# A 40-us tail of row tiles: identity passes moved ahead of the last mode, channel matmul first, spectra evacuated in two parts, a lag of three

## The chip, the cores and the metric

The kernel runs on one core of a Trainium2 chip. The metric is the device time of one execution in microseconds (us). The core's engines work side by side, each through its own instructions in program order: TensorE (PE, matrix passes), VectorE (DVE), ScalarE (ACT), GpSimd (POOL) and SyncE (SP), which here only issues DMAs. PE writes its results to PSUM, eight banks of 2 KB per partition; DVE and ACT move them from there to SBUF.

## The reference

Two stages follow each other. The first is sparse attention over batch 8, 8 heads, 576 positions, head size 64 (four heads with a local mask of 32 positions, four with a strided mask). Its output, seen as x of shape (8, 576, 512), goes into a spectral mixer:

```python
X = np.fft.rfft(x, axis=1)
Xr, Xi = (np.real(X[:, :n_modes]), np.imag(X[:, :n_modes]))        # 64 modes
Yr = np.einsum('bmd,mde->bme', Xr, w_r) - np.einsum('bmd,mde->bme', Xi, w_i)
Yi = np.einsum('bmd,mde->bme', Xr, w_i) + np.einsum('bmd,mde->bme', Xi, w_r)
Y[:, :n_modes] = Yr + 1j * Yi
y = np.fft.irfft(Y, n=S, axis=1)
u = x + y
return (u + np.maximum(u @ w_ch, 0.0)).astype(np.float32)
```

The mode weights w_r and w_i are 64 matrices of 512 x 512 each. The output is (8, 576, 512) in float32, 9.44 MB.

## The kernel before, in words

Every engine runs its instructions in the order in which the program text issues them; waits between engines are inserted where one reads what another writes, and PSUM accesses to the same bank of one tile are put in order. No planner reorders anything.

**The weight stream.** `w_fetch` (L181) has POOL issue two DMAs per mode and half of the channels, 256 KB each on arrival, 254 in all. They run from the start to about 402.5 us. `mode(slot, m)` does 16 small passes (L516, 128x16) for one mode. Slot 0 handles one half of the channels while the local attention runs, slot 1 the other half while `premix` runs. Eight modes share one PSUM tile y; after the eighth, L531 or L533 moves all eight to SBUF (slot 1 adds what slot 0 left and writes the spectra tile YT).

**Premix.** While slot 1 streams, `premix` computes for each row tile (b, t) the product x @ w_ch (into `v0`, through ACT L612) and a copy of x in row order (`xo`, through DVE L613). There are five row tiles per batch: t = 0 to 3 with 128 rows, and t = 4 with 64 rows, two batches of which share one tile. That makes 36 units in the tail: per batch (b,0), (b,1), then (b,4) for odd b, then (b,2), (b,3).

**Spectra.** For every 16 modes and four batches `spec_mm` transposes the spectra (L622, into tp) and multiplies them by w_ch (L625, into zp). `spec_out` then copies, per batch, 32 rows of zp to `zz` on ACT (L631) and 32 rows of tp to `yy` on DVE (L632). The last 16 modes can go through this only after mode 63; for them `spec_last` is called.

**The tail (L809 to L886).** New PSUM pools are opened: z with 2 banks, v with 3, u with 3. They take the place of the pools tp, sc, av and y, which are closed. A unit does, in this order:

- `unit_v0`: PE passes `v0` through the identity into a v bank (L827).
- `unit_v`: `rows_v` adds the inverse transform of `zz` (L638, for t = 4 two half passes L641); ACT takes relu of it into `rl` (L836). For the units of `pool_adds` (t = 1, 3, 4, except (7,3), 19 in all) POOL adds `xo` to `rl` (L839).
- `unit_u`: for the other 17 units PE passes `xo` through the identity into a u bank (L654); for all, the inverse transform of `yy` (L656, for t = 4 L659). DVE adds u and `rl` into `osb` (L851). SP issues the output DMA: one of 512 KB for two units (L865), two of 128 KB for t = 4 (L856), and single ones of 256 KB for the last two units (L860).

On PE the order is: three `unit_v0`, the last spectra, then for each i `unit_v0(i)` (from i = 3), `unit_v(i)`, `unit_u(i - 2)`. With three banks for v, the identity pass of unit i waits for the relu of unit i - 3; with three for u, unit i waits for the add of unit i - 3. `spec_out` of the next batch follows the unit with t = 1; the last spectra of batches 4 to 7 follow unit (3,1).

Of the kernel before, what the change touches and what calls it, by code (L numbers as in the profile page):

```python
# [12 lines left out]
AluOp = mybir.AluOpType  # L13
ACTF = mybir.ActivationFunctionType

B = 8
# [3 lines left out]
NM = 64  # L20
# [57 lines left out]
def kernel(  # L78
# [10 lines left out]
    nc = tc.nc  # L89
    PSUM = bass.MemoryType.PSUM  # L90
# [5 lines left out]
    pss = {}  # L96
    pctx = ctx.enter_context(ExitStack())

    def psum_pools(**bufs):
        pctx.close()  # L100
        pss.clear()
        for n, c in bufs.items():
            pss[n] = pctx.enter_context(
                tc.tile_pool(name="ps_" + n, bufs=c, space=PSUM)
            )

    def psum(kind, half=False):
        if half:
            return pss[kind].tile([128, 1024], F16, tag=kind, name=kind)
        return pss[kind].tile([128, 512], FP, tag=kind, name=kind)  # L110
# [15 lines left out]
    idn = cs["cI"]  # L126
# [8 lines left out]
    YS = {}  # L135
# [28 lines left out]
    w_chs = {}  # L164

    def w_fetch(n=1):
        for _ in range(n):
            i = len(w_tiles)
            if i >= 2 * NM:
                return  # L170
            half, m = 1 - i // NM, i % NM
            if i in GUEST:
                n, j = GUEST[i]
                if j == 0:
                    guests[n] = big.tile([128, 2, 4, DM], F16, tag=n, name="wt")
# [329 lines left out]
    def mode(slot, m):  # L505
        half = 1 - slot
        mi, mg = m % 8, m // 8
        if mi == 0:
            ypt[slot] = psum("y")
        yp = ypt[slot]  # L510
        yv = yp.rearrange("p (m e x) -> p m e x", m=8, e=4)
        wt = w_tiles[slot * NM + m]
        pr = ds(0, 128 if m else 64)
        for e in range(4):
            for c in range(4):
                nc.tensor.matmul(  # L516
                    yv[:, mi, e, :],
                    wt[pr, XC[c], ds(128 * e, 128)],
                    Xh[half][pr, c, :, :, m],
                    start=(c == 0),  # L520
                    stop=(c == 3),
                )
        if slot or m not in GUEST:
            w_fetch()
        if mi == 7:
            part = (slice(None), slice(None), mg // 2, slice(None), ds(8 * (mg % 2), 8))
            src = yp.rearrange("p (m e x) -> p e x m", m=8, e=4)
            if slot == 0:
                if m == 7:
                    spectra_tile("Y0")  # L530
                nc.scalar.activation(out=YS["Y0"][part], in_=src, func=ACTF.Copy)  # L531
            else:
                nc.vector.tensor_tensor(  # L533
                    out=YS["YT"][part], in0=src, in1=YS["Y0"][part], op=AluOp.add
                )
# [83 lines left out]
    def spec_mm(g, bq, tp, zp):  # L619
        for e in range(4):  # L620
            lhs = YS["YT"][:, e, g, ds(8 * bq, 8), :].rearrange("p x m -> p (x m)")
            nc.tensor.transpose(tp[:, ds(128 * e, 128)], lhs, idn)  # L622
        for e in range(4):
            lhs = YS["YT"][:, e, g, ds(8 * bq, 8), :].rearrange("p x m -> p (x m)")
            nc.tensor.matmul(  # L625
                zp, lhs, w_chs["n"][:, e, :], start=(e == 0), stop=(e == 3)
            )

    def spec_out(g, b, tp, zp):
        src, dst = ds(32 * (b % 4), 32), ds(32 * g, 32)  # L630
        nc.scalar.activation(out=zzs[b][dst], in_=zp[src, :], func=ACTF.Copy)  # L631
        nc.vector.tensor_copy(out=yys[b][dst], in_=tp[src, 0:512])  # L632
# [14 lines left out]
                skip_group_check=True,  # L647
            )

    def rows_u(b, t, up, add):  # L650
        cols = out_cols(t)
        if add:
            xo = xos[b][:, t, :] if t < 4 else xoh[b // 2]
            nc.tensor.matmul(up, idn, xo, start=True, stop=(t == 4))  # L654
        if t < 4:
            nc.tensor.matmul(up, cs["cA"][:, cols], yys[b], start=not add, stop=True)  # L656
            return
        for i in range(2):
            nc.tensor.matmul(  # L659
                up[ds(64 * i, 64), :],  # L660
                cs["cA"][:, cols],
                yys[b - 1 + i],
                start=not add,
                stop=True,
                skip_group_check=True,
            )
# [63 lines left out]
    dft(B - 1, 1)  # L730


    psum_pools(tp=2, sc=2, av=2, y=2)
    NMODES = [11, 9, 8, 8, 7, 7, 7, 7]
    for b in range(B):
        load(B + b + 3)
# [2 lines left out]
        ends = [lambda h=h: loc_scores(b, h, True) for h in (0, 2)]  # L739
# [8 lines left out]
        n = 0  # L748
        nm = NMODES[b]
        for mi in range(nm):  # L750
# [3 lines left out]
            n = upto  # L754
# [7 lines left out]
    xoh = [ptr.tile([128, DM], F16, name=f"xoh{i}") for i in range(4)]  # L762
    zzs = [ptr.tile([128, DM], F16, name=f"zz{i}") for i in range(B)]
    yys = [ptr.tile([128, DM], F16, name=f"yy{i}") for i in range(B)]
# [31 lines left out]
            spec_out(g, b, tp, zp)  # L796

    n = 0
    for m in range(NM):
        mode(1, m)  # L800
        upto = min(len(work), -(-len(work) * (m + 1) // 62))
        for w in work[n:upto]:
            w()
        n = upto
        if m >= 16 and m % 16 in (4, 8):
            spec(m // 16 - 1, 0 if m % 16 == 4 else 1)


    psum_pools(z=2, v=3, u=3)  # L809
    units = []  # L810
    for b in range(B):
        units += [(b, 0), (b, 1)]
        if b % 2:
            units.append((b, 4))
        units += [(b, 2), (b, 3)]
    held, vps, rls, osbs = {}, {}, {}, {}
    LAST = len(units) - 1

    def spec_last(bq):
        held[bq] = psum("z", half=True), psum("z")  # L820
        spec_mm(3, bq, *held[bq])

    def unit_v0(i):
        b, t = units[i]
        vps[i] = psum("v")
        v0 = v0s[b][:, t, :] if t < 4 else v0h[b // 2]
        nc.tensor.matmul(vps[i], idn, v0, start=True, stop=(t == 4))  # L827

    def unit_v(i):
        b, t = units[i]  # L830
        vp = vps.pop(i)
        rows_v(b, t, vp)
        if t % 2 == 0:
            rls[b, t] = rls[b, t + 1] = pw.tile([128, 2, DM], FP, tag="w", name="rl")
        rl = rls[b, t][:, t % 2, :]
        nc.scalar.activation(out=rl, in_=vp, func=ACTF.Relu)  # L836
        if pool_adds(b, t):
            xo = xos[b][:, t, :] if t < 4 else xoh[b // 2]
            nc.gpsimd.tensor_tensor(out=rl, in0=rl, in1=xo, op=AluOp.add)  # L839

    def pool_adds(b, t):
        return t in (1, 3, 4) and (b, t) != (B - 1, 3)

    def unit_u(i):
        b, t = units[i]
        up = psum("u")
        rows_u(b, t, up, add=not pool_adds(b, t))
# [3 lines left out]
        nc.vector.tensor_tensor(  # L851
            out=osb[:, t % 2, :], in0=up, in1=rls[b, t][:, t % 2, :], op=AluOp.add
        )
        if t == 4:
            for j in range(2):
                nc.sync.dma_start(  # L856
                    out[b - 1 + j, ds(512, 64), :], osb[ds(64 * j, 64), 0, :]
                )
        elif i >= LAST - 1:
            nc.sync.dma_start(  # L860
                out[b, ds(256, 256), :].rearrange("(p i) e -> p i e", i=2)[:, t % 2, :],
                osb[:, t % 2, :],
            )
        elif t % 2:
            nc.sync.dma_start(  # L865
                out[b, ds(128 * (t - 1), 256), :].rearrange("(p i) e -> p i e", i=2),
                osb,
            )

    for i in range(3):  # L870
        unit_v0(i)
    spec_last(0)
    spec_out(3, 0, *held[0])
    LAG = 2
    for i in range(len(units) + LAG):
        if i < len(units):
            b, t = units[i]
            if i > 2:
                unit_v0(i)
            unit_v(i)  # L880
            if t == 1 and b + 1 < B:
                if b + 1 == 4:
                    spec_last(1)
                spec_out(3, b + 1, *held[(b + 1) // 4])
        if i >= LAG:
            unit_u(i - LAG)  # L886


# [28 lines left out]
```

The softmax here doesn't subtract the row's maximum and nothing guards it: scores larger than these inputs give would overflow.

## Time and profile before

| | |
|---|---|
| median of 4 runs | 445.53 us (443.85 to 446.93) |
| profiled execution | 444.46 us, its span 442.7 us |
| weight DMAs | 81 MB with the inputs, to about 402.5 us |
| PE busy, whole span | 341.3 us (77%) |
| last mode starts | 402.60 us |
| first row pass (L638) | 407.11 us |
| last PE pass starts | 436.34 us |
| last DVE add ends | 437.93 us |
| last output DMA issued | 439.0 us |

The page says, for one profiled execution, how long each engine was busy, and cuts the span into 40 slices. The chain of waits goes back from the last instruction to what released each. The timeline lists an engine's instructions with their start, length and the idle time before. In these rows, "PE y L516 x16" is sixteen passes of line 516 into tile y; a length in the timeline includes the way through the array, so passes that start 0.216 us apart are shown as 0.38 us long. The granted clock is the share of full speed at which PE ran.

### The profile page before, as it was taken

To read this page: it belongs to the slowest core of one execution; us is meant where nothing else is said; L and a number is where in the kernel's file an instruction comes from. 1 tells how busy PE (TensorE), PEld (TensorE's weight loads), DVE (VectorE), ACT (ScalarE), POOL (GpSimd) and SP (SyncE) were. 2 spreads that over 40 slices of the span, in tenths; PEclk is the share of its full clock that TensorE was granted. 3 is DMA by queue.
4 is the path that set the end of the run, shared out by engine and by line. 5 is a ranking of instruction groups with operands and counts; after the bars stand their busy time and mean duration, and the time that the engine had idled before them with its cause. 6 is when DMAs were issued, how large, how long until landed. Compare 5 with 4: busy or idle time off the path is not lost.

```text
span 442.7 us, 12293 instructions
## 1 busy us (share of the span) xinstructions
PE 341.3 (77%) x5285; PEld 242.4 (55%) x5285; DVE 214.8 (49%) x461; ACT 187.9 (42%) x353; POOL 179.6 (41%) x326
## 2 busy tenths in 40 slices
PE   3878789769898795866865575978869787887994
PEld 2767677648676674654743344545545464543441
DVE  4787767835344424150511034345344543732895
ACT  2675667645554543343441311215114221332883
POOL 5243333433433443443443444434444444410773
PEclk9996889888898958595785568779577885978998
DMA  8999999999999999999999999999999999990687
GB/s 186 181 205 204 197 200 204 212 208 211 210 211 211 213 212 200 212 211 212 211 210 212 212 212 212 211 212 208 210 194 208 213 211 213 210 208 17 262 323 272
DMA packets 30758, 92.35 MB, mean 209 GB/s; under 512 B 5936, under 2 KB 6832, under 8 KB 30704
## 3 DMA queue, kind: packets, MB, share of 16 engines
q0 software_dynamic: 26608, 81.28, 93.9%
q1 hardware_dynamic: 3520, 9.90, 6.0%
q8 instruction: 42, 0.69, 0.6%
q10 hardware_dynamic: 576, 0.38, 0.3%
q14 instruction: 12, 0.10, 0.1%
HBM read 163.37 MB, written 9.44 MB: 390 GB/s over the span
## 4 chain that ended last, share of the span: by engine, by line
DMA 58%; PE 16%; issue 2%; ACT 1%; DVEq 0%; DVE 0%; ACTq 0%; POOLq 0%
DMA wt<-in_moe_w_i_dram 47%; DMA wt<-in_moe_w_r_dram 9%; PE y L516 3%; DMA qn<-in_k_dram 2%; PE v L827 2%; PE tp L364 2%; PE v L638 1%; PE u L656 1%; PE sc L410 1%; PE sc L426 1%; PE u L654 1%; PE y L483 1%; PE av L447 1%; PE z L625 1%; PE av L455 0%
## 5 line engine op out<-in xcount | busy, mean ns | idle before, releaser
L516 PE MATMUL y<-X,wt 128*128 128x16 f16 (+1 forms) x2048 | 82.8, 192 | 64.2 <-DMA wt<-in_moe_w_i_dram 62.5
L181 POOL DMA_DIRECT2D wt<-in_moe_w_r_dram x128 | 66.2, 517 | 128.3 <-DMA wt<-in_moe_w_r_dram 28.9
L516 PEld LDWEIGHTS <-wt 128*128 128x128 f16 (+1 forms) x2048 | 72.7, 103 | 77.3 <-issue 52.0
L181 POOL DMA_DIRECT2D wt<-in_moe_w_i_dram x126 | 65.1, 516 | 63.5 <-DMA wt<-in_moe_w_i_dram 39.0
L603 PE MATMUL sc<-w_cp,xT 128*128 128x512 f16 (+1 forms) x160 | 54.7, 473 | 0.7 <-DVE xT L575 0.7
L612 ACT ACTIVATE v<-sc 128x512 f16<-128x512 f32 x32 | 19.0, 597 | 82.3 <-PE sc L603 82.2
L440 ACT ACTIVATE PL<-sc 128x480 f16<-128x480 f32 (+1 forms) x48 | 27.4, 579 | 40.7 <-PE sc L426 39.4
L613 DVE COPY xo<-tp 128x512 f16<-128x512 f16 x32 | 22.1, 692 | 45.3 <-PE tp L611 45.3
L219 DVE TENSOR_TENSOR xb<-av,rec 90x256 f16<-90x256 f32 (+2 forms) x80 | 36.0, 450 | 2.8
L218 DVE RECIPROCAL rec<-av 90x4 f32<-90x4 f32 (+2 forms) x80 | 14.7, 183 | 43.1 <-PE av L455 30.0
L371 DVE COPY qT<-tp 128x576 f16<-128x576 f16 x16 | 12.1, 759 | 45.6 <-PE tp L364 41.5
L229 ACT ACTIVATE v<-tp 128x640 f16<-128x640 f16 (+1 forms) x24 | 19.4, 807 | 26.6 <-PE tp L398 23.5
L364 PE MATMUL tp<-cI_s,qn 64*64 64x64 f16 x864 | 26.2, 210 | 4.7 <-issue 3.0
L329 ACT ACTIVATE PS<-sc 90x360 f16<-90x360 f32 (+1 forms) x48 | 22.8, 489 | 9.3 <-PE sc L322 8.6
L851 DVE TENSOR_TENSOR osb<-u,rl 128x512 f32<-128x512 f32 x36 | 23.3, 687 | 6.0 <-ACT rl L836 3.0
L839 POOL TENSOR_TENSOR rl<-rl,xo 128x512 f32<-128x512 f32 x15 | 17.3, 1156 | 21.2 <-ACT rl L836 20.7
L364 PEld LDWEIGHTS <-qn 64*64 64x64 f16 x864 | 20.5, 122 | 9.8 <-issue 4.7
L603 PEld LDWEIGHTS <-xT 128*128 128x128 f16 (+1 forms) x160 | 15.0, 112 | 16.6 <-issue 8.3
L254 PE MATMUL tp<-cI_s,qn 72*128 72x72 f16 x256 | 15.4, 211 | 10.7 <-DMA qn<-in_v_dram 7.9
L483 PEld LDWEIGHTS <-xb 108*128 108x128 f16 (+2 forms) x176 | 17.2, 115 | 11.5 <-DVE xb L219 6.1
L410 PE MATMUL sc<-cMl_s,cI_s 128*128 128x480 f16 (+1 forms) x48 | 21.9, 456 | 1.6 <-ACT X L229 1.6
L611 PEld LDWEIGHTS <-xT 128*128 128x128 f16 (+1 forms) x160 | 15.1, 117 | 13.7 <-issue 7.9
(92 smaller groups left out, 650.4 us busy)
## 6 DMA issues: line engine op xcount, KB each, us to landing
wt<-in_moe_w_r_dram POOLq DMA_DIRECT2D x128, 256.0 KB, 9.4
wt<-in_moe_w_i_dram POOLq DMA_DIRECT2D x126, 256.0 KB, 9.6
out_dram<-osb SPq DMA_DIRECT2D x15, 512.0 KB, 2.8
qn<-in_v_dram POOLq DMA_DIRECT2D x16, 288.0 KB, 10.7
qn<-in_q_dram POOLq DMA_DIRECT2D x16, 288.0 KB, 10.9
qn<-in_k_dram POOLq DMA_DIRECT2D x16, 288.0 KB, 10.7
out_dram<-osb SPq DMA_DIRECT2D x8, 128.0 KB, 2.5
w_ch<-in_moe_w_ch_dram POOLq DMA_DIRECT2D x1, 512.0 KB, 11.7
```

The lines of the kernel that those rows point to most:

```text
L181: nc.gpsimd.dma_start(wt[ds(64 * ri, 64)], src[m, ds(256 * half, 256), :].rearrange("(p c) e -> p c e", c=4),)
L219: nc.vector.tensor_tensor(out=dst, in0=val.rearrange("p h (q c) -> p h c q", c=4), in1=rec[0:n, 0:pieces] .to_broadcast((n, pieces, 64)) . ...
L229: nc.scalar.activation(out=out, in_=in_, func=ACTF.Copy)
L329: nc.scalar.activation(out=PS[0:n, ds(POFF[t], 4 * n)], in_=scp[0:n, 0 : 4 * n], func=ACTF.Exp, scale=SCALE,)
L364: nc.tensor.transpose(tp[ds(64 * hp, 64), ds(64 * i, 64)], qn[ds(64 * hp, 64), vi, ds(64 * (9 * g + i), 64)], idn[ds(64 * hp, 64), ds(64 * ...
L410: nc.tensor.matmul(scp[:, 0 : n * times].rearrange("p (h x) -> p h x", h=times), idn, mask_rows("cMl", n, times), start=True, stop=False,)
L440: nc.scalar.activation(out=dst, in_=src, func=ACTF.Exp, scale=SCALE)
L483: nc.tensor.matmul(xp[:, ds(192 * cp, 192)], xb[b][0:n, base + t, ds(128 * cp, 128)], F[0:n, t, :], start=(i == 0), stop=(i == len(tiles) ...
L516: nc.tensor.matmul(yv[:, mi, e, :], wt[pr, XC[c], ds(128 * e, 128)], Xh[half][pr, c, :, :, m], start=(c == 0), stop=(c == 3),)
L603: nc.tensor.matmul(vp[pr, :], xT[:, ch, cols], w_chs["cp"][:, ch, :], start=(ch == 0), stop=(ch == 3),)
L613: nc.vector.tensor_copy(out=xo[pr].rearrange("p (h q c) -> p h q c", h=2, c=4), in_=tp[pr, 0:512].rearrange("p (h c q) -> p h q c", h=2, c=4),
L851: nc.vector.tensor_tensor(out=osb[:, t % 2, :], in0=up, in1=rls[b, t][:, t % 2, :], op=AluOp.add)
```

## The change

- `psum_pools` no longer forgets older pools. Pool y is opened first and stays open to the end; in the tail, v and u (3 banks each) take the place of tp, sc and av, and the last spectra use the two y banks.
- The eighth group of slot 1 is evacuated in two parts: six modes after the sixth, two after the eighth.
- The loop over modes stops at 62. Then three units do their identity passes for v and for u (`v_early`, `u_early`: six passes, as unit (0,1) is no longer added by POOL), and only then does mode 63 run.
- `spec_last` does the four channel matmuls first, then the four transposes.
- `pool_adds` leaves out (0,1) and adds (2,2) and (4,2): 20 units.
- `u_rows` follows `v_rows` at a distance of three units for i from 4 to 31, and of two before and after.
- The first two units send their output singly. The second half of the last t = 4 tile and the last unit's output are issued on ACT's queue.

```diff
@@ mode
-        if mi == 7:
-            part = (slice(None), slice(None), mg // 2, slice(None), ds(8 * (mg % 2), 8))
-            src = yp.rearrange("p (m e x) -> p e x m", m=8, e=4)
+        ends = {7: 8}
+        if slot and mg == 7:
+            ends = {5: 6, 7: 2}
+        if mi in ends:
+            n = ends[mi]
+            m0 = mi + 1 - n
...
+            src = yp.rearrange("p (m e x) -> p e x m", m=8, e=4)[:, :, :, ds(m0, n)]
@@ pools
-    psum_pools(tp=2, sc=2, av=2, y=2)
+    psum_pools()
+    pss["y"] = ctx.enter_context(tc.tile_pool(name="ps_y", bufs=2, space=PSUM))
+    psum_pools(tp=2, sc=2, av=2)
...
-    for m in range(NM):
+    for m in range(NM - 1):
...
-    psum_pools(z=2, v=3, u=3)
+    psum_pools(v=3, u=3)
@@ tail
+    def pool_adds(b, t):
+        if (b, t) in ((0, 1), (B - 1, 3)):
+            return False
+        return t in (1, 3, 4) or (b, t) in ((2, 2), (4, 2))
+
     def spec_last(bq):
-        held[bq] = psum("z", half=True), psum("z")
-        spec_mm(3, bq, *held[bq])
+        zp = psum("y")
+        tp = psum("y", half=True)
+        held[bq] = tp, zp
+        for dst in (zp, tp):
+            for e in range(4):
+                lhs = YS["YT"][:, e, 3, ds(8 * bq, 8), :].rearrange("p x m -> p (x m)")
+                if dst is tp:
+                    nc.tensor.transpose(tp[:, ds(128 * e, 128)], lhs, idn)
+                else:
+                    nc.tensor.matmul(
+                        zp, lhs, w_chs["n"][:, e, :], start=(e == 0), stop=(e == 3)
+                    )
+    def u_early(i):
         b, t = units[i]
+        ups[i] = psum("u")
+        if not pool_adds(b, t):
+            nc.tensor.matmul(ups[i], idn, x_rows(b, t), start=True, stop=(t == 4))
...
-                nc.sync.dma_start(
+                (nc.scalar if b == B - 1 and j else nc.sync).dma_start(
...
-        elif i >= LAST - 1:
-            nc.sync.dma_start(
+        elif i < 2 or i >= LAST - 1:
+            (nc.scalar if i == LAST else nc.sync).dma_start(
...
     for i in range(3):
-        unit_v0(i)
+        v_early(i)
+        u_early(i)
+    mode(1, NM - 1)
     spec_last(0)
     spec_out(3, 0, *held[0])
-    LAG = 2
-    for i in range(len(units) + LAG):
-        if i < len(units):
-            b, t = units[i]
-            if i > 2:
-                unit_v0(i)
-            unit_v(i)
-            if t == 1 and b + 1 < B:
...
+    done = 0
+    for i in range(len(units)):
+        v_rows(i)
+        b, t = units[i]
+        if t == 1 and b + 1 < B:
...
+        lag = 3 if 3 < i < LAST - 3 else 2
+        while done <= i - lag:
+            u_rows(done)
+            done += 1
+    while done <= LAST:
+        u_rows(done)
+        done += 1
+    psum_pools()
```

`v_rows` and `u_rows` are `unit_v` and `unit_u` of before; each issues its unit's identity pass itself where it has not been issued early.

More of the change, by code (lines that the diff above doesn't have):

```diff
@@ L100, in psum_pools @@
         pctx.close()
-        pss.clear()
         for n, c in bufs.items():
@@ L524, in mode @@
             w_fetch()
-        if mi == 7:
-            part = (slice(None), slice(None), mg // 2, slice(None), ds(8 * (mg % 2), 8))
-            src = yp.rearrange("p (m e x) -> p e x m", m=8, e=4)
+        ends = {7: 8}
[4 more added lines that the diff above has]
+            m0 = mi + 1 - n
+            part = (
+                slice(None),
+                slice(None),
+                mg // 2,
+                slice(None),
+                ds(8 * (mg % 2) + m0, n),
+            )
+            src = yp.rearrange("p (m e x) -> p e x m", m=8, e=4)[:, :, :, ds(m0, n)]
             if slot == 0:
@@ L648, in rows_v, with rows_u @@
             )
-    def rows_u(b, t, up, add):
+    def rows_u(b, t, up, fresh):
         cols = out_cols(t)
-        if add:
-            xo = xos[b][:, t, :] if t < 4 else xoh[b // 2]
-            nc.tensor.matmul(up, idn, xo, start=True, stop=(t == 4))
         if t < 4:
-            nc.tensor.matmul(up, cs["cA"][:, cols], yys[b], start=not add, stop=True)
+            nc.tensor.matmul(up, cs["cA"][:, cols], yys[b], start=fresh, stop=True)
             return
@@ L662, in rows_u @@
                 yys[b - 1 + i],
-                start=not add,
+                start=fresh,
                 stop=True,
@@ L815, with x_rows, v_early @@
         units += [(b, 2), (b, 3)]
-    held, vps, rls, osbs = {}, {}, {}, {}
+    held, vps, ups, rls, osbs = {}, {}, {}, {}, {}
     LAST = len(units) - 1
-    def spec_last(bq):
-        held[bq] = psum("z", half=True), psum("z")
-        spec_mm(3, bq, *held[bq])
-    def unit_v0(i):
+    def x_rows(b, t):
+        return xos[b][:, t, :] if t < 4 else xoh[b // 2]
+    def pool_adds(b, t):
+        if (b, t) in ((0, 1), (B - 1, 3)):
+            return False
+        return t in (1, 3, 4) or (b, t) in ((2, 2), (4, 2))
+    def spec_last(bq):
+        zp = psum("y")
[9 more added lines that the diff above has]
+                        zp, lhs, w_chs["n"][:, e, :], start=(e == 0), stop=(e == 3)
+                    )
+    def v_early(i):
         b, t = units[i]
@@ L827, in unit_v0, with v_rows @@
         nc.tensor.matmul(vps[i], idn, v0, start=True, stop=(t == 4))
-    def unit_v(i):
+    def v_rows(i):
         b, t = units[i]
+        if i not in vps:
+            v_early(i)
         vp = vps.pop(i)
@@ L837, in unit_v, with u_rows @@
         if pool_adds(b, t):
[L838 to L844, printed above, removed]
-        b, t = units[i]
-        up = psum("u")
-        rows_u(b, t, up, add=not pool_adds(b, t))
+            nc.gpsimd.tensor_tensor(out=rl, in0=rl, in1=x_rows(b, t), op=AluOp.add)
+    def u_early(i):
+        b, t = units[i]
+        ups[i] = psum("u")
+        if not pool_adds(b, t):
+            nc.tensor.matmul(ups[i], idn, x_rows(b, t), start=True, stop=(t == 4))
+    def u_rows(i):
+        b, t = units[i]
+        if i not in ups:
+            u_early(i)
+        up = ups.pop(i)
+        rows_u(b, t, up, pool_adds(b, t))
         if t % 2 == 0:
@@ L855, in unit_u @@
             for j in range(2):
-                nc.sync.dma_start(
+                (nc.scalar if b == B - 1 and j else nc.sync).dma_start(
                     out[b - 1 + j, ds(512, 64), :], osb[ds(64 * j, 64), 0, :]
                 )
-        elif i >= LAST - 1:
-            nc.sync.dma_start(
-                out[b, ds(256, 256), :].rearrange("(p i) e -> p i e", i=2)[:, t % 2, :],
+        elif i < 2 or i >= LAST - 1:
+            (nc.scalar if i == LAST else nc.sync).dma_start(
+                out[b, ds(128 * (t - t % 2), 256), :].rearrange(
+                    "(p i) e -> p i e", i=2
+                )[:, t % 2, :],
                 osb[:, t % 2, :],
@@ L870 @@
     for i in range(3):
-        unit_v0(i)
+        v_early(i)
+        u_early(i)
+    mode(1, NM - 1)
     spec_last(0)
     spec_out(3, 0, *held[0])
-    LAG = 2
-    for i in range(len(units) + LAG):
-        if i < len(units):
-            b, t = units[i]
-            if i > 2:
-                unit_v0(i)
-            unit_v(i)
-            if t == 1 and b + 1 < B:
[L882 to L886, printed above, removed]
+    done = 0
+    for i in range(len(units)):
+        v_rows(i)
+        b, t = units[i]
+        if t == 1 and b + 1 < B:
+            if b + 1 == 4:
+                spec_last(1)
+            spec_out(3, b + 1, *held[(b + 1) // 4])
+        lag = 3 if 3 < i < LAST - 3 else 2
[6 more added lines that the diff above has]
+    psum_pools()
 _INS = ['q', 'k', 'v', 'moe_w_r', 'moe_w_i', 'moe_w_ch']
```

## The prediction

> **What bounds the kernel now.** I read the page first, then the chain of waits over the last 48 us, then each engine's timeline there, then windows of the granted clock. The page gives the span and what the span is made of.
>
> ```profile
> span 442.7 us, 12293 instructions
> DMA  8999999999999999999999999999999999990687
> ```
>
> The second line has the DMA engines' busy tenths in 40 slices: nearly full through the first 36 (weights stream in), and only then does anything else set the time. The profiled execution took 444.46 us: 442.7 of span and 1.76 around it. It lies 1.07 under the median of 445.53, so sums are made against 444.46 and set beside the median at the end. The change touches nothing ahead of 397 us, where the weight stream bounds, so only the last 40 us can move. The chain of waits there (start, length, what):
>
> ```profile
> 391.75 10.71 DMA wt<-in_moe_w_i_dram
> 402.60 0.64 PE y L516 x16
> 403.23 1.28 PE v L827 x3
> 404.51 0.43 PE z L622 x4
> 404.94 1.51 PE z L625 x4
> 406.47 0.59 ACT zz L631
> 407.11 0.39 PE v L638
> ```
>
> The last weights land, the last mode runs, and 4.5 us pass before the first row pass L638 at 407.11. After that the chain is PE pass after PE pass, 0.22 us each, to 436.34: PE bounds the tail. It had one gap worth naming, 0.22 us at 409.05, where L638 waited for the second zz. The groups from 405 us on show how near the others are:
>
> ```profile
> L851 DVE TENSOR_TENSOR osb<-u,rl 128x512 f32<-128x512 f32 x36 | 23.3, 687 | 6.0 <-ACT rl L836 3.0 <-POOL rl L839 1.9 <-PE u L656 0.8
> L836 ACT ACTIVATE rl<-v 128x512 f32<-128x512 f32 x36 | 20.1, 598 | 4.1 <-PE v L638 3.5 <-PE v L641 0.4
> L654 PE MATMUL u<-xo,cI_s 128*128 128x512 f16 x17 | 6.5, 382 | 0.0
> ```
>
> DVE is busy 23 us with adds and 3.4 with yy copies out of 29, so it is next in line. Last, the clock in half-microsecond windows (columns: window, length, PE, weight loads, DVE, ACT, POOL, clock, DMA share, GB/s):
>
> ```profile
> 402.00:402.50 0.50, 0.00 (x0) 0.00 (x0) 0.00 (x0) 0.00 (x0) 0.00 (x0) 1.00 0.00 0
> 402.50:403.00 0.50, 0.41 (x14) 0.44 (x15) 0.00 (x0) 0.00 (x0) 0.00 (x0) 0.67 0.00 0
> 403.00:403.50 0.50, 0.50 (x10) 0.22 (x8) 0.16 (x1) 0.00 (x0) 0.00 (x0) 0.50 0.00 0
> ...
> 406.00:406.50 0.50, 0.43 (x2) 0.14 (x1) 0.00 (x0) 0.03 (x1) 0.00 (x0) 0.92 0.00 0
> ```
>
> Between about 402.7 and 406.1 PE runs at half clock: a 512-column pass takes 0.43 us there and 0.216 outside.
>
> **The change, part by part.**
>
> **Six passes ahead of the last mode.** PE is empty from 400.61 (mode 62 issued) to 402.60. Six passes at 0.216 end at 401.91, so mode 63 starts at 402.60 as now. This takes the three L827 passes (1.28 us of the chain) from behind the mode. If the clock is already half at 400.6, six passes are 6 x 0.427 = 2.56, end at 403.17 and push the last mode 0.57 us. Their banks were last read by the copies of the last premix, over at 400.25, so nothing else holds them.
>
> **Spectra in two parts.** The whole eviction L533 took 0.69 at 403.34. Two modes of eight are 128 elements; between the 128x64 copies L561 (0.22) and 0.69 for 512 a straight line gives an estimate of 0.29 us (bounds 0.18, the L579 copy, and 0.69); I take 0.29. The first part, six modes, costs about 0.55 on DVE near 398.4. DVE's next work is at 399.55, and mode 62, which writes the same bank and may wait for it, waits for weights to 400.14 anyway; without that cover it costs PE 0.55.
>
> **Channel matmul first.** z now follows the eviction at once and ACT starts on it while PE transposes. Eviction ends 403.34 + 0.29 = 403.63, PE starts z at 403.70. At full clock four z passes take 1.03 (as at 417.71), so zz starts at 404.76, takes 0.58, and the first row pass starts at 405.40: 1.71 us earlier than 407.11. At half clock z takes 1.70, the first row pass starts at 406.07: 1.04 earlier. Transposes (0.22 or 0.43) and the yy copy (0.42) hide under zz and the first three row passes; if they did not, u would start at most 0.4 late.
>
> **Identity passes in the stream.** L654 now has 17 in the stream. Units (0,0) and (0,2) go ahead of the mode, (2,2) and (4,2) move to POOL, (0,1) comes off POOL but its pass is one of the six: four passes x 0.216 = 0.87 less. Against it stands ACT. From the first row pass, relu 0, relu 1 and the second zz follow at 0.52, 0.52 and 0.58, and the row pass of (1,0) needs that zz: about 2.15 us after the first row pass, what it is now (407.11 to 409.27). So one saved pass buys nothing. With no u pass in the slot of unit 4 (the lag grows to three there), the next v pass waits for relu 2 about 0.36 more. Stalls go from 0.22 to about 0.75; the stream is 0.87 - 0.53 = 0.34 shorter.
>
> **POOL and the lag.** POOL has 20 adds instead of 19, 20 x 1.156 = 23.1 of 29 us. (2,1), (2,2), (2,3) follow each other, relus come 0.8 apart, so the third runs 0.7 late; a lag of three leaves 2.4 us, so it is hidden. At lag two, DVE would wait about 0.5, as its 1.9 us on POOL now do, still off PE's path. At the end three adds follow POOL's (7,4) add: DVE ends at 437.93, 1.21 after PE's last pass ends at 436.72. The catching up puts two u units into the slot of unit 32, so POOL is done before PE and I get 0.95: 0.25 less.
>
> **Outputs.** SP issues the last four one after another; the columns are those of the windows above:
>
> ```profile
> 436.76 1.11 SPq L856 DMA_DIRECT2D out_dram<-osb  x2
> 437.97 1.03 SPq L860 DMA_DIRECT2D out_dram<-osb  x2
> ```
>
> ```profile
> 438.00:439.00 1.00, 0.00 (x0) 0.00 (x0) 0.00 (x0) 0.00 (x0) 0.00 (x0) 1.00 0.93 232
> 439.00:440.00 1.00, 0.00 (x0) 0.00 (x0) 0.00 (x0) 0.00 (x0) 0.00 (x0) 1.00 0.97 332
> ```
>
> Two of the four go to ACT's queue, behind the last relu with nothing after them; the last one is issued 0.51 us sooner. But the engines are 93% and 97% busy when it is issued. [...] I take 0, bounds -0.5 and +0.8. Splitting the first pair sends output earlier into idle engines: 0.
>
> **Which clock.** [...]
>
> ```profile
> 399.27:402.68 3.41, 0.96 (x24) 0.74 (x22) 0.70 (x1) 0.59 (x1) 0.00 (x0) 1.00 0.13 26
> 402.68:406.10 3.42, 3.42 (x27) 1.72 (x27) 1.53 (x3) 0.00 (x0) 0.00 (x0) 0.50 0.02 5
> 136.44:139.86 3.42, 2.44 (x71) 2.03 (x72) 1.42 (x2) 1.08 (x3) 1.58 (x3) 1.00 1.06 211
> 221.78:225.19 3.41, 2.28 (x31) 1.46 (x30) 0.00 (x0) 3.12 (x8) 1.55 (x3) 1.00 1.06 213
> ```
>
> A window with 0.96 us of PE was enough to halve it; one with 2.44 was also followed by half clock, one with 2.28 by full. The changed window holds 0.96 + 1.30 = 2.26, on the edge. And in the window after, now 3.42 of 3.42 busy, about 0.6 (eviction) and 0.24 (zz) would be idle, so a halved clock may last one window more, to 409.5.
>
> Sum, clock full: -1.71 - 0.34 - 0.25 = -2.3, hence 442.2. Clock half to 409.5: the row pass of (1,0) comes at 409.5 instead of 409.27 (eight passes at 0.427 after 406.07), then three passes fewer, 0.65, with no ACT stall, and 0.25 at the end: +0.25 - 0.65 - 0.25 = -0.65, hence 443.8. [...] Since the windows lie differently in each execution, the runs will hold both, as the four runs of before do (443.85 to 446.93, where one more half window costs up to 3.41 / 2 = 1.7 us). I forecast the middle: **443.0 us**, 2.5 below the median.
>
> **Rivals.** (1) The halved clock takes the head back in most executions: -0.65, or entered half with the mode pushed 0.57. For it: the edge above; against it: six passes fill two thirds of the gap. 443.8 to 445, say 444.4. (2) The output engines set the end: late outputs queue up, and 0.8 us comes back: 443.8. For it 0.93 and 0.97 above; against it 0.65 share at 435.0, so they were not behind. (3) Slower: the clock does not return after the head, because the ACT-paced start leaves PE gaps and no window is busy enough. Each further half window costs 1.7 in a PE-bound stream: 443.8 + 3 x 1.7 = 448.9. It decides from two further windows on (447.2). Against it: PE is gapless from 409.5. (4) The passes are not early, because PE waits for their banks: then they cover the shorter eviction as three do now, and only the order of z (0.43) and the end (0.25) are saved: 443.8. The copies end at 400.25, so this is unlikely and counted within (1).
>
> **How the numbers follow.** Forecast 0.55, (1) with (4) 0.27, (2) 0.10, (3) 0.08. About 0.5% (2.2 us) is what a measurement of this kernel can tell from none. The forecast is mostly past that line, (1) and (2) within it: faster 0.53, same 0.39, slower 0.08. Range: the full-clock sum with 0.5 at the outputs, 441.7, to the half-clock one with most of another window, 445.2. The forecast's own range is 441.7 to 443.9.
>
> **What would show it.** Row pass of unit 0 at 405.4 (full) or 406.1 (half) instead of 407.11; six identity passes between 400.6 and 402; a 128x128 eviction near 0.29; L654 down by four in the stream; a PE gap near unit 5 waiting for ACT; last DVE add 1.0 after PE. I am wrong if the mode starts late, if the clock is half beyond 409.5, or if the last bytes leave later than 3 us after the last add.

## The result

The changed kernel takes 442.77 us in the median (441.52 to 444.90, 42 runs) against 444.66 us (443.11 to 446.93, 61 runs) for the kernel before. The ratio is 0.9963, 95% interval 0.9954 to 0.9972: 1.65 us less (the two medians are 1.89 apart). A second measurement of the same two kernels, among the experiments below, gave 0.9974 (0.9957 to 0.9992). The forecast was 443.0 us. Its sum starts from the profiled execution of before, 444.46 us, which lies 0.2 us under the median of 61 runs, and takes 1.46 us off. The "2.5 below the median" beside it was against four runs, whose median of 445.53 was 0.9 us high. The prediction put at 0.5% what can be told from none; with this many runs 0.37% could be told.

The profiled execution took 443.62 us. First the page, then the chain of waits from the mode before the last on:

```profile
span 441.8 us, 12290 instructions
```

```profile
400.28 0.64 PE y L515 x16
400.92 0.43 PE v L854
401.35 0.43 PE u L873
401.78 0.43 PE v L854
402.20 0.43 PE u L873
402.63 0.43 PE v L854
403.06 0.43 PE u L873
403.48 0.44 PE y L515 x16
403.95 0.30 DVE YT L543
404.30 1.05 PE y L846 x4
405.37 0.59 ACT zz L641
406.01 0.81 PE v L648 x3
```

The lines of the kernel have moved: L854 is the identity pass of v (L827 before), L873 that of u (L654), L846 the channel matmul (L625), L648 the row pass (L638). The six passes stand between the last two modes, but at 0.43 us each: PE was at half clock just there. (The chain places the last mode at 403.48; PE's timeline has its first pass at 403.28, and that value is used below.) The clock is the eighth column:

```profile
397.10:400.52 3.42, 2.26 (x37) 1.50 (x34) 1.95 (x3) 1.18 (x2) 0.00 (x0) 1.00 0.56 110
400.52:403.94 3.42, 3.39 (x36) 1.60 (x32) 0.00 (x0) 0.00 (x0) 0.00 (x0) 0.50 0.04 8
```

A window with 2.26 us of PE, none of it the six passes, was followed by half clock; the passes then filled the next one (3.39 of 3.42), and everything from the eviction on ran at full clock. The groups from 404 us on:

```profile
L884 DVE TENSOR_TENSOR osb<-u,rl 128x512 f32<-128x512 f32 x36 | 23.9, 689 | 2.5 <-ACT rl L865 0.8 <-ACT zz L641 0.5 <-PE u L663 0.5
L865 ACT ACTIVATE rl<-v 128x512 f32<-128x512 f32 x36 | 20.4, 597 | 3.8 <-PE v L648 2.1 <-DVE osb L884 0.6 <-PE v L651 0.4
L873 PE MATMUL u<-xo,cI_s 128*128 128x512 f16 x13 | 4.9, 381 | 0.0
```

DVE no longer waits for POOL (1.9 us before), and the stream has 13 of the u passes instead of 17. Last the end, from the timeline, and the output transfers with their size and median time from issue to landing:

```profile
435.23 0.47 SPq L889 DMA_DIRECT2D out_dram<-osb  x1
435.23 0.55 ACTq L889 DMA_DIRECT2D out_dram<-osb  x1
435.83 1.04 SPq L893 DMA_DIRECT2D out_dram<-osb  x1
436.43 0.48 ACTq L893 DMA_DIRECT2D out_dram<-osb  x1
```

```profile
out_dram<-osb SPq DMA_DIRECT2D x3, 256.0 KB, 3.2
out_dram<-osb ACTq DMA_DIRECT2D x1, 256.0 KB, 4.3
```

Two of the three on SP are the first units' outputs, issued at 407.84 and 409.05, when little other output was under way; they took 3.2 and 2.4 us. The third, issued at 435.83, took 4.7, so it was no faster than ACT's 4.3. The last output's issue is over at 436.91 instead of 439.0, 2.1 us sooner, but the span ends only 0.9 us sooner. Cut at three events (start of the last mode, first row pass, end of the last DVE add), the profiles compare so:

| profile | last mode to row pass | row pass to last add | last add to end of span |
|---|---|---|---|
| before | 4.51 | 30.82 | 4.76 |
| changed | 2.73 | 30.38 | 5.45 |

The head gives 1.78 us, the stream 0.44, and the end takes 0.69 back. The last mode itself started 0.54 us late because of the half clock: the last packet of its weights was over at 402.28, and in the profiles in which the last mode waits it starts 0.41 to 0.47 after that, mostly 0.46. That explains the profile: -1.78 - 0.44 + 0.69 = -1.53, with the last mode 0.68 later (402.60 to 403.28) -0.85, which is the difference of the spans.

### The profile page after: what moved, and what is told of

Its sections match the earlier page's. It is cut to its first block, busy times and chain, and to the rows that moved or that the text cites. A ratio compares the mean times of both kernels' runs of the same rounds, so it can differ in the third digit from the quotient of the medians.

```text
span 441.8 us, 12290 instructions
## 1 busy us (share of the span) xinstructions
PE 340.6 (77%) x5284; PEld 242.8 (55%) x5284; DVE 215.4 (49%) x462; ACT 189.1 (43%) x353; POOL 180.6 (41%) x327
## 4 chain that ended last, share of the span: by engine, by line
DMA 75%; PE 13%; DVE 4%; issue 3%; ACT 2%; POOL 0%; DVEq 0%; POOLq 0%; ACTq 0%
DMA wt<-in_moe_w_i_dram 53%; DMA wt<-in_moe_w_r_dram 13%; DMA qn<-in_v_dram 5%; DMA qn<-in_q_dram 4%; PE v L854 2%; PE u L663 2%; PE v L648 2%; DVE xb L218 1%; DVE kz L260 1%; PE u L873 1%; PE sc L482 1%; PE y L515 1%; PE tp L253 1%; PE tp L292 1%; ACT v L228 1%
## 5 line engine op out<-in xcount | busy, mean ns | idle before, releaser
L613 PE MATMUL sc<-w_cp,xT 128*128 128x512 f16 (+1 forms) x160 | 52.6, 458 | 0.7 <-DVE xT L585 0.7
L867 POOL TENSOR_TENSOR rl<-rl,xo 128x512 f32<-128x512 f32 x16 | 18.3, 1157 | 18.8 <-ACT rl L865 18.5
L613 PEld LDWEIGHTS <-xT 128*128 128x128 f16 (+1 forms) x160 | 14.7, 110 | 16.1 <-issue 7.6
L641 ACT ACTIVATE zz<-av 32x512 f16<-32x512 f32 x24 | 14.1, 588 | 21.0 <-PE av L635 20.8
L425 PE MATMUL sc<-qT,kz 128*128 128x160 f16 (+1 forms) x160 | 22.4, 267 | 0.0
```

The lines of the kernel that those rows point to most:

```text
L425: nc.tensor.matmul(scp[:, ds(col, n)], kzs[par][:, hp, ds(s0, 128)], qTs[par][:, ds(s0, n)], start=False, stop=(i == len(todo) - 1),)
L613: nc.tensor.matmul(vp[pr, :], xT[:, ch, cols], w_chs["cp"][:, ch, :], start=(ch == 0), stop=(ch == 3),)
```

## The experiments

All ratios are to the kernel before, measured on the same chip; the changed kernel's 0.9963 and 0.9974 are the marks. Going by the intervals, two of these kernels can be told apart from about 0.2% on.

**The six passes behind the last mode.**

```diff
+    mode(1, NM - 1)
     for i in range(3):
         v_early(i)
         u_early(i)
-    mode(1, NM - 1)
```

> The changed kernel with mode 63 ahead of the six identity passes instead of behind them. My theory: the passes pay because they lie in the wait for the last weights; behind the mode they cost 6 x 0.216 = 1.3 us at full clock (2.6 at half) and hide only the 0.29 us eviction, so the median goes up by 0.7 to 2.0 us against the changed kernel, and the first row pass comes near 406.5 or later. Rival (a pushed last mode gives the gain back, as in the profiled execution, where the mode started at 403.48): within 0.3 us of the changed kernel.

445.74 us, ratio 1.0014 (1.0003 to 1.0025): 0.51%, or 2.3 us, above the changed kernel, and no better than the kernel before. The chain of its profile:

```profile
402.88 0.64 PE y L515 x16
403.52 0.43 PE v L854
...
405.66 0.43 PE u L873
406.08 1.55 PE y L846 x4
407.63 0.02 issue
407.65 0.59 ACT zz L641
408.25 0.04 issue
408.29 0.81 PE v L648 x3
```

5.41 us from the last mode to the row pass instead of 2.73. The six passes stand on the path at half clock, and so does the channel matmul behind them (1.55 us). The 2.3 us are more than the 0.7 to 2.0 expected, and the rival, that a pushed mode gives the gain back, falls: the place of the passes decides the result. At full clock this head would take about 3.5 us by the steps of the profiles (0.47 for the mode, 6 x 0.216, 1.05 for z, 0.64 to the row pass), 0.75 more than 2.73; this is an estimate. The median lost 2.3, so most executions probably met half clock here, as the profiled one did. All the other edits together, with six passes here where the kernel before has three, gain nothing.

**The head's other two edits undone** (eviction in one part, transposes first; the passes stay early).

```diff
-            ends = {5: 6, 7: 2}
+            ends = {7: 8}
...
-        for dst in (zp, tp):
+        for dst in (tp, zp):
```

> The changed kernel with the last eight modes evacuated in one part, and transposes ahead of the channel matmuls, as before the change; the six passes stay ahead of the last mode. By the prediction's steps both are on the path now that nothing else covers them: 0.69 - 0.29 = 0.40 us for the eviction, and 0.22 (full clock) or 0.43 (half) for the transposes, so 0.6 to 0.8 us above the changed kernel. Rival (the executions' spread in the weight stream hides it, or the start is paced by ACT): within 0.3 us.

444.09 us, ratio 0.9987 (0.9971 to 1.0003), some 1.1 us above the first mark, 0.6 above the second; only the first difference is clear of the intervals. Its chain:

```profile
402.68 0.65 PE y L515 x16
...
403.42 0.70 DVE YT L543
404.13 0.05 issue
404.17 0.40 PE y L844 x4
404.57 0.88 PE y L846 x4
...
406.11 0.81 PE v L648 x3
```

3.43 us against 2.73, at full clock in both: 0.70 us, made of 0.40 for the eviction (0.70 against 0.30) and about 0.30 for the transposes. In the profile these two edits are worth what was expected, 0.6 to 0.8. At half clock they would not have been with the passes behind the mode: three of them took 1.28 us in the kernel before and ended after the eviction.

**Four passes ahead instead of six, and six with two repeated.** The first does the u passes of units (0,1) and (0,2) in the stream; the second does them early and once more in the stream, so that PE is as busy ahead of the last mode as with six. Its stream does two passes of work that is not needed.

```diff
@@ four ahead
         v_early(i)
-        u_early(i)
+        if i == 0:
+            u_early(i)
@@ two repeated
...
         up = ups.pop(i)
+        if i in (1, 2):
+            nc.tensor.matmul(up, idn, x_rows(b, t), start=True, stop=False)
         rows_u(b, t, up, pool_adds(b, t))
```

> The changed kernel with four passes ahead of the last mode (three v and the first u) instead of six; the other two u passes go back into the stream. Theory: at half clock six passes take 2.56 us from 400.76 and push the last mode to 403.48, four take 1.7 us and end at 402.5, so executions that are at half clock there gain up to 0.8 us less the two passes in the stream (0.43, partly under ACT's pace); at full clock it is the same or 0.4 slower. Median 0.0 to 0.4 us lower, and the slowest executions come down. Rival (the number of passes in the stream is what counts): 0.4 us higher.

> The changed kernel, six passes ahead of the last mode as there, but the u passes of units (0,1) and (0,2) are done a second time in the stream. So PE is as busy ahead of the last mode as with six passes, and the stream is as long as with four. Theory of the clock (six passes keep PE busy enough for full clock more often, and that is what four lost, 0.85 us): as the changed kernel, within 0.3 us, at most the 0.43 us of the two passes above it. Theory of the stream (the two passes in the stream are the loss): as the kernel with four passes, 0.7 us or more above the changed kernel.

Four passes: 444.35 us, ratio 0.9982 (0.9970 to 0.9993). Two repeated: 442.57 us, ratio 0.9955 (0.9938 to 0.9972, 8 runs). So two passes more in the stream cost nothing that the times show; in both profiles the row pass to the last add takes 30.60 us, 0.22 more than 30.38, half of the two passes' 0.43; that the other half falls into the time in which ACT paces PE fits this, but was not tried apart. With four passes the hoped-for gain did not come. That four are worse because the clock is halved more often with less PE work in the wait fits the pair, but no run shows it: the one profile with four shows full clock throughout, a head of 2.73 us and an end of 4.93, and the interval overlaps that of the second mark. It stays open whether four are worse at all.

**Three passes ahead of each of the last two modes.**

```diff
-    for m in range(NM - 1):
+    for m in range(NM - 2):
...
     for i in range(3):
+        u_early(i)
+    mode(1, NM - 2)
+    for i in range(3):
         v_early(i)
-        u_early(i)
     mode(1, NM - 1)
```

> The changed kernel with the three u passes ahead of mode 62 and the three v passes ahead of mode 63, so that each group fills one wait for weights. Theory: at half clock three passes take 1.28 us and fit before the last weights, so the last mode is never pushed (0.88 us in the profiled execution of the changed kernel), and PE is as busy in sum; the median falls by 0.2 to 0.5 us, the slowest executions by 0.8. Rival: the push is rare or given back at once, because a mode pushed at half clock meets a clock that is full sooner: within 0.2 us.

443.10 us, ratio 0.9958 (0.9941 to 0.9975): not to be told from the changed kernel. PE's timeline shows what is left in the way:

```profile
400.87 0.81 PE L873 MATMUL u<-xo,cI_s 128*128 128x512 f16 x3 [0.46 <-ACT v0h L622]
401.51 0.64 PE L515 MATMUL y<-X,wt 128*128 128x16 f16 x16
401.99 0.81 PE L854 MATMUL v<-v,cI_s 128*128 128x512 f16 x3
403.39 0.64 PE L515 MATMUL y<-X,wt 128*128 128x16 f16 x16 [0.59 <-DMA wt<-in_moe_w_i_dram]
```

The three u passes wait 0.46 us for ACT's last premix copy, whose bank they take. The last mode then waits for its weights, as wanted. But the clock went to half later in this profile, from 406.1 to 409.6, and row pass to last add took 31.23 us.

**A lag of two throughout.**

```diff
-        lag = 3 if 3 < i < LAST - 3 else 2
+        lag = 2
```

> The changed kernel with a lag of two units throughout. Theory: PE bounds the stream and the waits of DVE on POOL are off its path, so the middle does not change; the gap of 0.4 us near 408.4, where a v pass waits for a relu because no u pass is in the slot, goes, and the end loses the 0.25 us that the catching up gave: within 0.3 us. Rival (the lag is what took DVE's waits off the path, and earns a large part of the gain): 0.8 us or more slower.

443.45 us, ratio 0.9966 (0.9955 to 0.9977). DVE's adds from 400 us on:

```profile
L884 DVE TENSOR_TENSOR osb<-u,rl 128x512 f32<-128x512 f32 x36 | 23.2, 687 | 4.0 <-POOL rl L867 2.0 <-ACT rl L865 0.9 <-ACT zz L641 0.5
```

The 2.0 us of waits for POOL are back and the time has not moved (30.47 us from row pass to last add): they are off PE's path. The rival, that the lag earns a large part, falls.

**Every output on SP.**

```diff
-                (nc.scalar if b == B - 1 and j else nc.sync).dma_start(
+                nc.sync.dma_start(
...
-            (nc.scalar if i == LAST else nc.sync).dma_start(
+            nc.sync.dma_start(
```

> The changed kernel with every output DMA on SP. Theory of the interleaved end: with two queues the last transfers share the 16 engines and all land late (4.3 us from issue to landing against 3.2 before), so one queue is 0.2 to 0.6 us faster although the last DMA is issued some 0.5 us later. Theory of issue time: 0.5 us slower. The sum of the prediction, which put 0 there: within 0.2 us.

443.72 us, ratio 0.9971 (0.9959 to 0.9984), between the two marks. In its profile the last add ends at 437.23; SP's timeline behind it:

```profile
436.21 1.20 SPq L889 DMA_DIRECT2D out_dram<-osb  x2
437.51 1.05 SPq L893 DMA_DIRECT2D out_dram<-osb  x2
```

The last issue is over 1.33 us after the last add instead of 0.52, and the span ends 5.98 us after it instead of 5.45. Each of the last two lands 3.7 us after its issue instead of 4.7 and 4.3, but is issued later by more than that. The end does not come sooner with one queue, so interleaving is not what made it late; whether two queues save a few tenths, as this one profile suggests, the times can't tell.

**Unit (7,4) earlier, and the last two outputs merged.** The first puts the 64-row unit ahead of (7,0), its outputs on SP. The second writes the last two units in one transfer of 512 KB; the third does that with ACT issuing nothing; the fourth joins the second to three passes ahead of each mode.

```diff
@@ (7,4) earlier
+        if b == B - 1:
+            units += [(b, 4), (b, 0), (b, 1), (b, 2), (b, 3)]
+            continue
...
@@ merged
-        elif i < 2 or i >= LAST - 1:
-            (nc.scalar if i == LAST else nc.sync).dma_start(
+        elif i < 2:
+            nc.sync.dma_start(
```

> The changed kernel with unit (7,4) ahead of (7,0) instead of between (7,1) and (7,2), its two outputs on SP, the last unit's on ACT. Theory: after the last DVE add 5.4 us pass in the changed kernel's profile (4.8 before) because transfers in 64 rows and 2 KB packets queue up at the end; with (7,4) done four units earlier only two transfers are left behind the last add, and the end comes 0.3 to 0.7 us sooner. Rival (the time after the last add is the latency of the last transfer): within 0.2 us.

> The changed kernel itself once more, as the mark for the other three on this chip: ratio to the kernel before 0.996 to 0.997. In its profile, first row pass 2.7 us after the last mode starts if the clock is full there, and 5 us or more between the last DVE add and the end of the span.

> The changed kernel with the last two units' outputs in one transfer of 512 KB in packets of 4 KB on SP instead of two of 256 KB in packets of 2 KB. Theory (the bytes still to go after the last add, 950 KB, and the packet size set the end; 2 KB packets move at 230 to 330 KB per us, 4 KB ones at 400): 0.2 to 0.5 us sooner. Rival (latency from the last issue sets it, and the first half now waits 0.6 us longer): 0 to 0.4 us later.

> As the one before, and the second half of the last 64-row tile on SP too, so ACT issues no output. Theory of bytes: within 0.2 us of it. Theory of two queues (their interleaving is what makes the last bytes late): up to 0.4 us sooner. Theory of issue time: 0.5 us later, because the last transfer stands behind two of 0.55 us on SP.

> The merged last output together with three u passes ahead of mode 62 and three v passes ahead of mode 63. If both theories hold, 0.3 to 0.8 us below the changed kernel, ratio 0.9945 to 0.9957; if only the merge or neither does, within 0.3 us of the changed kernel.

| kernel | median us (runs) | ratio (95% interval) | last add to end, us |
|---|---|---|---|
| (7,4) earlier | 443.12 (22) | 0.9971 (0.9960 to 0.9981) | 5.71 |
| changed, again | 443.75 (12) | 0.9974 (0.9957 to 0.9992) | 5.13 |
| merged | 442.78 (12) | 0.9959 (0.9944 to 0.9974) | 5.52 |
| merged, all on SP | 442.52 (12) | 0.9963 (0.9948 to 0.9978) | 5.22 |
| merged, three and three | 442.53 (12) | 0.9961 (0.9945 to 0.9976) | 5.04 |

In their profiles none ends sooner after the last add than those with the changed kernel's output order do (4.93 to 5.45 us, below), and none can be told from the changed kernel by its time. The theory that the queue of small packets sets the end, so that fewer or larger ones shorten it, is not borne out. Nor is there a version here that beats the changed kernel.

What these kernels did not vary on purpose is how many bytes are still to go at the last add. The rows run from there to the end of the span, with the rate in GB/s as the last column, for the kernel before and the changed one:

```profile
437.93:442.69 4.76, 0.00 (x0) 0.00 (x0) 0.00 (x1) 0.00 (x0) 0.00 (x0) 0.74 0.54 173
436.39:441.84 5.45, 0.00 (x0) 0.00 (x0) 0.01 (x1) 0.00 (x0) 0.00 (x0) 0.65 0.51 167
```

That is 0.82 MB before and 0.91 MB in the changed kernel. It is 1.10 MB with every output on SP and 1.19 MB with (7,4) earlier, the two longest ends (5.98 and 5.71 us); in the other variants 0.89 to 0.98.

In the profile with (7,4) earlier the clock fell to half after the head, not before it:

```profile
401.30:404.70 3.40, 2.01 (x26) 1.26 (x26) 0.71 (x3) 0.58 (x1) 0.00 (x0) 1.00 0.02 5
404.70:408.15 3.45, 3.45 (x9) 1.27 (x9) 1.10 (x2) 2.76 (x5) 0.03 (x1) 0.51 0.00 0
```

Row pass to last add took 31.34 us against 30.38. From the first to the last pass it is 0.85 of this, half of the 1.7 us that a window at half clock can cost (half of 3.4 us, an estimate); that ACT holds PE up in those first units anyway fits this. The other 0.12 lies behind the last pass, and belongs to the new order.

## Why the prediction was right, and where not

**The head at full clock: right.** Predicted 1.71 us, measured 1.78 (4.51 to 2.73), in eleven profiles of the changed kernel and its variants to within 0.01, wherever the passes were early and the other two edits were in. The eviction took 0.29, as the straight line gave it; zz started 0.64 before the row pass (0.64), z took 1.05 (1.03). The two experiments that undo parts of it (2.68 and 0.70 us in their profiles) show that both are needed.

**What the early passes seem to earn is mostly clock.** The experiment with the old eviction and order has a head of 3.43 us at full clock, with no pass behind the mode. Three passes there would end about 1.12 us after the mode starts (0.47 + 3 x 0.216), before that eviction does (1.44), so at full clock they would have cost the kernel before nothing. This is an estimate, but by it only 0.70 of the 1.78 us come from the eviction and the order, and 1.08 from the half clock that the head of before had and the new one has not. All twelve profiles with passes in the wait run from the eviction to the first row pass at full clock, and the two without them, before and the passes behind the mode, start that stretch at half. No run keeps PE busy in the wait with other work, which would have told the two apart. The prediction's sum set a half-clock head against a full-clock one, so it holds this gain, but it names the three passes on the chain as the thing that goes.

**The pushed mode: right in kind and size.** "If the clock is already half at 400.6" was put at 0.57 us; the changed kernel's profile has it at 0.54, and the one with the merged output at 0.46. In the other seven with all six passes ahead of the last mode, the mode waits for its weights. That 2.26 us of PE, named as undecided, was also in the window that halved the clock is chance: the prediction meant a window that holds the six passes, and this one ends before them.

**Half clock over z and the first units: not seen.** I had set the case of 443.8 apart from 442.2 by 1.65 us: 0.67 for z at half clock and about 0.98 for the first units. No profile with the passes early shows both, so whether the gaps after the last mode (0.6 and 0.24 us) can keep a halved clock down was not put to the test there. In the profile of before, over the whole span, 31 of the 32 half-clock windows that PE did not fill were followed by another at half clock (the last section has the count); the 409.5 us of the sum is shown by no run. Where the clock was half at the head (the changed kernel and the merged output), it fell before the passes began, and was back by z. Where a half-clock window fell into the first units instead (three profiles, from 404.6 to 409.6), it cost 0.85 us of PE, near the 0.98.

**The stream: 0.44 instead of 0.59.** First to last pass went from 29.23 to 28.99 us (0.24 for 0.34), the last add from 1.59 to 1.39 us after the start of PE's last pass (0.20 for 0.25). The stall near unit 5 is there: no pass is due for about 0.4 us up to 408.79, where PE waits for relu. That POOL's waits are off the path held, as the lag of two shows.

**Outputs: the mis-sized term.** I took 0, with bounds of -0.5 and +0.8. In eight profiles with the changed kernel's output order the end of the span lies 4.93 to 5.45 us behind the last add, 5.22 in the mean, against 4.76 in the one profile of before: +0.46. The issue time saved does not show in the times (0.9971 with every output on SP lies between the marks, 0.9963 and 0.9974). No run shows the +0.8 itself: it is an estimate, the 256 KB of one unit at 0.33 MB per us (332 GB/s in the row from 439.00); what the profiles show in its place is the +0.46. The rival "the output engines set the end" named the sign; its 0.8 us was nearly twice the size. Against it the prediction read a share of 0.65 at 435.0 as engines that were not behind. That reading was wrong; the outputs of the kernel before took, from issue to landing:

```profile
DMA to landing us min/median/max: 2.3/2.8/4.7
```

The 4.7 is the one issued at 432.76, and the next two of 512 KB took 4.3 and 4.1. So outputs were queued up over the last 5 us of the stream before the change as well, and in the changed kernel (4.8, 4.5 and 4.4 from 431.65 on). The stream now ends sooner, with 0.09 MB more to go; at 0.33 MB per us that is 0.26 us, an estimate, of the 0.46. Undoing the lag, the second queue, the packet size and the place of (7,4) did not remove the growth, and 4.76 is one execution; the bytes fit it, but no experiment has shown that they are the cause.

Put together: -1.78 - 0.44 + 0.46 = -1.76 with the mode on time, -1.22 with the mode pushed, about -0.9 with the first units at half clock. The measured -1.65 (and -1.16 in the second measurement) fits a mix of these. The forecast's 1.46 us was the middle between -2.3 and -0.65, in the belief that executions would divide between full and half clock. In the profiles the head and the stream stay near the full-clock sum, and it is mostly the end, put at 0, that takes the rest back. That the middle was met is luck in this; the gain of the head and the stream is not.

**The signs of being wrong.** Two of the three came up although the forecast held. The mode started late in the profiled execution. The last bytes left more than 3 us after the last add: the last output packet was over 4.0 us after it, but 3.5 in the kernel before, so that sign could not tell the two apart.

**What makes the executions differ: wrong.** I gave the spread of the runs to the place of the clock's windows. They do lie differently: half clock begins at 402.68 us in the profile of before, at 400.52 in that of the changed kernel and at 404.70 in that with (7,4) earlier, which are not whole windows of 3.41 us apart, and the changed kernel's second profile has its six passes 0.22 us apart, at full clock. But in the fourteen profiles the last packet of the weights is over anywhere from 401.20 to 403.64 us, 2.4 us apart, before the last mode has run, and the span follows: 40.5 us behind it in the kernel before, 38.7 to 40.2 in the kernels with early passes. So the spread of runs (3.4 us in the changed kernel) seems to lie mostly in the weight stream, as far as single profiles of different kernels can say; what moves its end was not tried.

## What to carry to other kernels

When a stream of loads ends a phase, move work that needs none of it into the wait before the last piece, and then look at what that work used to cover: at half clock the shorter eviction and the new order pay only once no pass stands in front of them. Such a wait can cost more than its own length: in both profiles without work in it, the head behind it began at half clock, 0.43 us per 512-column pass instead of 0.22. Size the work so that it fits at half clock too, or expect to pay part of it back (0.54 us in the changed kernel's profile). An engine wait that the groups view shows in us (here DVE on POOL, 2 us; the ratio is 0.9966 with it and 0.9963 without) is worth nothing until the chain of waits goes through it.

## What the runs showed of the hardware

The same PE work costs differently by the clock it meets: each of the six passes ahead of the last mode took 0.43 us in two profiles and 0.22 in the other seven with all six there. In the profile of before, cut into 127 windows of 3.41 us from 3.32 to 436.82 us, the granted clock is 1.00 or 0.50 in every one. Of the 74 at full clock with a successor, the 25 in which PE was busy for at most 2.44 us were followed by half clock 19 times, the 49 with 2.46 us or more never. Of the 52 at half clock, the 20 that PE filled (3.41 us busy) were followed by full clock 18 times, the other 32 once.

In the tails, a 3.4-us window with 2.26 us of PE ahead of the passes was followed by half clock, one with 2.01 us was so ahead of the first units, and in both cases full clock was back after one window that PE filled (3.39 of 3.42 and 3.45 of 3.45 us). But in the profile of the head's two edits undone the window from 400.76 to 404.17 held only 1.96 us, and the clock stayed full; together with the 2.28 us (full) and 2.44 us (half) of the kernel before, no amount of PE time below 2.46 us divides the cases, and what else counts stays open. With the passes behind the mode, the window from 400.5 to 403.9 held 1.59 us at half clock, and the clock stayed half for another.

In these profiles the time of an output from issue to landing went with how much output was under way, not with the issuing engine. In the changed kernel's profile 512 KB on SP took 2.6 to 3.0 us up to the one issued at 430.30, and 4.8, 4.5 and 4.4 us from 431.65 on; the last two of 256 KB took 4.7 on SP and 4.3 on ACT. The last issue came 2.1 us sooner than before, and the span ended only 0.9 us sooner.
